# Three moved steps in an mLSTM and feed-forward kernel: chunk 3's mask, the copies of b, and the last piece of w_out

## The chip, the cores and the metric

The kernel runs on one core of a Trainium2 chip. The metric is the device time of one launch in microseconds (us). PE is TensorE, DVE is VectorE, ACT is ScalarE, POOL is GpSimd and SP is the engine that only issues transfers.

## The reference, cut to what matters

Two blocks follow each other. The first is a recurrent cell over 4 batches of 8 heads, 768 steps, head width 40. The second is a feed-forward block on its 3072 rows of 320 numbers:

```python
for t in range(S):
    m_new = np.maximum(f_gate[:, :, t] + m, i_gate[:, :, t])
    f_stab = np.exp(f_gate[:, :, t] + m - m_new)
    i_stab = np.exp(i_gate[:, :, t] - m_new)
    m = m_new
    C = f_stab[:, :, None, None] * C + i_stab[:, :, None, None] * np.einsum('bhd,bhe->bhde', vt, kt)
    n = f_stab[:, :, None] * n + i_stab[:, :, None] * kt
    h_tilde = np.einsum('bhde,bhe->bhd', C, qt)
    nq = np.einsum('bhd,bhd->bh', n, qt)[:, :, None]
    denom = np.maximum(np.abs(nq), 1.0)
    o = 1.0 / (1.0 + np.exp(-o_gate[:, :, t]))
    y[:, :, t] = o * h_tilde / denom
...
h = np.maximum(x @ w_in, 0.0)
return (h * h @ w_out).astype(np.float32)
```

Here `x` is `y` with the heads laid side by side (320 columns), `w_in` is 320 x 2048 and `w_out` is 2048 x 320. Both weights arrive as 64-bit numbers.

## The kernel before, in words

**Chunks.** The 3072 rows are cut into 24 chunks of 128 steps (6 chunks in each batch). A chunk is computed in a parallel form. Its scores k·q (`scores`) are multiplied by a matrix of weights `W` = exp(A + b), where A is the running sum of the log decays and b a number for each key; the product is `P` (`weighted`, line 552). `P` times the values, plus the state C of the chunks before, gives the numerators (`attend`, later `attend_begin` and `attend_end`), which are divided by the denominators (`normalise`, later `normalise_turned`).

**How W is made.** `load_A` brings A, spread over all partitions, into the tile `A_bc`. `mask` (line 425) lets GpSimd fill the places where the key is later than the query with -1e30. `weigh` then runs eight exponentials on ScalarE (line 467) and at last `values` multiplies the values by a column of W on GpSimd (`vw`, line 487). From chunk 8 on another layout is used, where the exponentials (line 461) take b from `b_R`. That is `b_T` with its halves of partitions exchanged, made by four ScalarE copies (line 1200).

**Weights.** `w_in` and `w_out` arrive in 18 pieces: pieces 0 to 9 are of `w_in`, 10 to 17 of `w_out`. A piece goes through the class `Rounding`. `fetch` loads it, `words` runs two ScalarE activations on it (`mag`, line 211, and `low`, line 213), and `join` runs three VectorE instructions (lines 222, 226, 227) and one GpSimd addition (line 231), then fetches another piece if one is left. `step` is `words` for the next piece and `join` for the oldest one.

**Two phases, one order written out by hand.** Every engine carries out its instructions in the order in which the program names them; no scheduler moves them.

- The first phase is the loop over `u`, from 0 to 7 (line 1137). Two values of `u` belong to one chunk s = 2 + u // 2: the even one does `scores`, `weighted` and `weigh(s + 1)`; the odd one does `attend`, `normalise` and the transposes of chunk s + 1. In each `u` a part of the first feed-forward product runs (`ffn1`, lines 799 and 810) into PSUM banks named `h_ps`, three of which exist. The next `u` begins with `relu_half` (line 823), which empties two of them. Joins of weight pieces fill in between: piece 4 in `u` = 0, pieces 5, 6 and 7 in `u` = 1.
- The second phase is the loop over the list `parts`, counted by `n` (line 1217); chunk s = 6 + n // 4 is spread over four values of `n`. It forms both feed-forward products with seven products of blocks instead of eight (`ffn1_begin`, `ffn1_open`, `ffn1_rows`, `ffn1_close`, `ffn2_fast`), except for the first two chunks of rows, which take the plain `ffn2` (line 836). `ffn1_begin` in `n` = 0 multiplies one block into each of two banks (line 966), lets ScalarE copy them (`r_sb`, line 979) and multiplies a second block on top. In `n` = 4 come the scores and `P` of chunk 7, and half of `ffn2` on the first rows. In `n` = 5 come `attend_begin(7)` and `attend_end(7)`, and between the two a one-element VectorE instruction (line 628) that TensorE waits for; then the other half of that product. At the start of `n` = 5 the buffers of `Rounding` are given back and `T` and `S` take their place; `T` holds differences of blocks of `w_out` (lines 864 to 871).

`LAST` tells for `n` = 0 to 4 how many pieces must have been joined by the end of that part.

Of the kernel before, what the change touches and what calls it, by code (L numbers as in the profile page):

```python
# [29 lines left out]
def kernel(  # L30
# [27 lines left out]
    nc = tc.nc  # L58
# [4 lines left out]
    PR = H // 2  # L63
# [190 lines left out]
    b_T = consts.tile([P, B, NB, H], F32)  # L254
    eA_T = consts.tile([P, B, NB, H], F32)
    b_R = consts.tile([P, B, NB, 2, PR], F32)
# [44 lines left out]
    HALVES = slice(0, DP), slice(DP, 2 * DP)  # L301
# [148 lines left out]
    def weigh(s, masked=False):  # L450
        b, c = divmod(s, NB)
        d = st[s]
        A, n = d["A"], H // len(d["A"])
        d["W"] = flat_c[:, H * P * (s % 2) : H * P * (s % 2 + 1)].rearrange("p (h t) -> p h t", t=P) if s < W_IN else A[0]
        if s < X_SQ:
            d["dec"] = prep.tile([P, H], F32, name="dec")
        if len(A) == 1 and not masked:
            mask(s)
        for x in range(PR if s >= ROT else 0):
            for own, to in enumerate((slice(DP, P), slice(P, 2 * P))):  # L460
                nc.scalar.activation(  # L461
                    A[0][:, x, to], A[0][:, x, to], AF.Exp, bias=b_R[:, b, c, own, x : x + 1],
                )
        for i in range(len(A) if s < ROT else 0):
            hh = slice(i * n, (i + 1) * n)
            for h in range(n):
                nc.scalar.activation(
                    d["W"][:, i * n + h, :], A[i][:, h, :], AF.Exp, bias=b_T[:, b, c, i * n + h : i * n + h + 1],
                )
            if s < X_SQ:  # L470
                nc.scalar.activation(d["dec"][:, hh], A[i][:, :, P - 1], AF.Exp)
        values(s)
# [346 lines left out]
    def relu_half():  # L819
        if "half" in st:  # L820
            hs, g4 = st.pop("half")
            for i, h in enumerate(hs):
                nc.scalar.activation(g4[:, :, i, :], h[:], AF.Relu)
            st.setdefault("relu", []).append(g4)
# [214 lines left out]
    def ffn1_square():  # L1039
        if "open" in st:  # L1040
# [4 lines left out]
            nc.scalar.activation(g4[:, :, :, P0], g4[:, :, :, P0], AF.Square)  # L1045
            nc.scalar.activation(g4[:, :, :, P1], g4[:, :, :, P1], AF.Square)

    def do(f, s):
        if 0 <= s < NT:
            f(s)  # L1050
# [86 lines left out]
    for u in range(8):  # L1137
        s = 2 + u // 2
        relu_half()
        if u % 2 == 0:  # L1140
            if u == 0:
                ffn1(0, 0)
            else:
                turn_rows(s - 1)
                scores(s)
                ffn1(u // 4, u % 4)
            if u == 2:
                rounding.words()
            weighted(s)
            if u == 0:  # L1150
                rounding.step()
            if u == 2:
                mask(s + 1)
                rounding.join()
                rounding.join()
                weigh(s + 1, masked=True)
                rounding.words()
            else:
                weigh(s + 1)
                square_half()  # L1160
        else:
            load_A(s + 2)
            for r in {1: (4,), 3: (5, 6), 5: (7,), 7: ()}[u]:
                load(r)
            if u == 5:
                for r in range(4, 8):
                    half_tanh(r)
            attend(s)
            if u == 3:
                square_half()  # L1170
            rounding.join()
            normalise(s)
            for r in {5: (8,), 7: (9,)}.get(u, ()):
                load(r)
            for r in {5: (7,), 7: (8,)}.get(u, ()):
                pair_up(r)
            if u > 4:
                load_o(2 * s)
                load_o(2 * s + 1)
            transposes(s + 1)  # L1180
            rounding.words()
            ffn1(u // 4, u % 4)
            square_half()
        if u < 4:
            load_o(4 + u)
        while rounding.done < NEXT[u]:
            rounding.step()
        if u in WIN_SUMS:
            sums_of_win(WIN_SUMS[u])
# [4 lines left out]

    for m in range(2):
        for own in range(2):
            x = PR * (m ^ own ^ 1)
            nc.scalar.copy(b_R[HALVES[m], :, :, own], b_T[HALVES[1 - own], :, :, x : x + PR])  # L1200
    spread_slots(1)
    banks.close()
    ps_h = ctx.enter_context(tc.tile_pool(name="ps_h", bufs=5, space=PSUM))
# [6 lines left out]
    for g in range(1, NG):  # L1210
        parts += [(2, g, i) for i in range(4)]
        if g + 2 < NG:
            parts += [(1, g + 2, i) for i in range(4)]
    LAST = (17, 17, 18, 18, 18)
    assert LAST[-1] == len(pieces)

    for n, (which, g, i) in enumerate(parts):
        s, at = 6 + n // 4, n % 4
        if n == 5:
            brought.close()  # L1220
            late = ctx.enter_context(tc.tile_pool(name="late", bufs=1, side="right"))
        even = s >= 8 and s % 2 == 0
        fast = which == 1
        if at == 0:
            if s < 8 or even:
                do(scores, s)
            if even:
                do(turn_kq, s + 1)
            if s < 8 or even:
                do(weighted, s)  # L1230
        if at == 1:
            do(attend_begin, s)
            if even:
                do(lambda s: scores(s, ("h", "h")), s + 1)
            if fast:
                ffn1_rows(g, 0, True)
            do(attend_end, s)
            do(decays, s + 1)
            do(mask, s + 1)
            if n > 4 and not even and not fast:  # L1240
                do(turn_kq, s + 1)
            do(decay_C, s + 1)
            if s > X_SQ and not fast and not even:
                do(turn_squares, s - 1)
            do(store_num, s)
            do(load_num, s)
            do(load_squares, s + 2)
            if even:
                do(load_A, s + 2)
        if 5 <= n < 8:  # L1250
            sums_of_weights(n - 5)
        if n == 6:
            sums(1, slice(0, NPAIR), (1, 2))
        if n == 8:
            sums_of_weights(3)
            sums(1, slice(0, NPAIR), (3,))
        if n == 9:
            sums(1, slice(0, NPAIR), (4,))
        if which == 2 and i == 3 and g == NG - 2:
            sums(g + 1, slice(0, NPAIR), (2,))  # L1260
        if which == 2 and g > 1 and i < 2:
            sums(g, slice(0, NPAIR), (3 + i,))
        if n == 0:
            ffn1_begin(g)
            sums_of_x(g)
            sums_of_win(2)
        if at == 3 and s >= 8 and s % 2 == 0 and s // 2 - 1 < NG:
            sums_of_x(s // 2 - 1)
        if at == 2 and not fast:
            if even:  # L1270
                do(turn_squares, s - 1)
            if n > 4:
                do(scale_q, s + 1)
        if at == 3:
            if s % 4 == 3:
                for r in range(s + 1, min(s + 5, NT)):
                    half_tanh(r)
        if fast:
            if i % 2:
                ffn1_close(g, i // 2, i == 1)  # L1280
                if at == 1 and g > 2:
                    do(turn_kq, s + 1)
                    do(turn_squares, s - 1)
            else:
                ffn1_open(g, i // 2)
                if i == 0 and g > 2:
                    sums(g - 1, slice(0, NPAIR), (2,))
            if at == 2 and g > 2:
                do(scale_q, s + 1)
        elif g == 0:  # L1290
            ffn2(g, *divmod(i, 2))
        else:
            ffn2_fast(g, i)
        if at == 2:
            do(lambda s: weigh(s, masked=True), s + 1)
            ffn1_square()
            if n < 4:
                do(turn_kq, s + 1)
                do(scale_q, s + 1)
            if even:  # L1300
                do(weighted, s + 1)
            do(normalise_turned, s)
            do(store_rows, s)
            if not even:
                do(load_A, s + 2)
            if s > 6:
                do(load_o, s + 5)
            do(load_rows, s)
            if s == 6:
                do(pair_up, s + 3)  # L1310
        if s > 6 and at == (3 if even else 2):
            do(pair_up, s + 3)
        if s > 6 and at == 3:
            if s == 7:
                load(s + 3)
            do(load, s + 4)
        if n in (9, 25):
            spread_slots(2 + n // 25)
        if at == 0:
            ffn1_square()  # L1320
        if n < 5:
            while rounding.done < LAST[n]:
                rounding.step()
# [30 lines left out]
```

## Time and profile before

| what | value |
|---|---|
| median of 3 runs | 500.82 us (500.54 to 502.58) |
| the profiled execution | 498.15 us, of which 496.4 us is the span from its first to its last instruction |
| TensorE clock granted | 1.000 |
| PE busy | 487.0 us (98%) |
| DVE, ACT, POOL busy | 346.3, 241.3, 224.5 us |

The span is the time from the first to the last instruction of the profiled execution; 1.75 us lie outside it. The median of the timed runs is 2.67 us above the profiled execution, so differences are worked out inside the profile and then set against the median. A row of the timeline gives start, duration, engine, line, operation and operands; in square brackets stands how long the engine was idle before it, and what ended that wait. Rows of one engine can overlap by about 0.1 us, because an instruction starts while its predecessor finishes.

### The profile page before, as it was taken

The numbers are of one execution on the slowest core, as the hardware profiler recorded it, in microseconds if no ns is written. First come the engines' busy times: TensorE is split into PE (matmuls) and PEld (weight loads), VectorE is DVE, ScalarE is ACT, GpSimd is POOL, SyncE is SP. The second block draws the span as 40 slices with busy tenths as digits, with TensorE's granted clock in tenths as the row PEclk, the third lists the DMA queues.
The fourth block names the chain that finished last, engine by engine and source line by source line (L and its number), as shares of the span: only waits on it lengthen the run. The fifth ranks groups of instructions, "written<-read, shape, count | busy, mean of one in ns | idle before, by whom it ended". The sixth has DMA issues, their size and how long they took to land.

```text
span 496.4 us, 15227 instructions
## 1 busy us (share of the span) xinstructions
PE 487.0 (98%) x6169; PEld 452.5 (91%) x6169; DVE 346.3 (70%) x700; ACT 241.3 (49%) x530; POOL 224.5 (45%) x317
## 2 busy tenths in 40 slices
PE   9999999999999999999999999999999999999997
PEld 4877878897799999999999999999999999999997
DVE  8598969868977677767866866866866956735441
ACT  3657888754612551581561670561861560423300
POOL 3265744531489458458549438448544030020000
PEclk9999999999999999999999999999999999999999
DMA  9999797756597597688678578677766532200000
GB/s 188 207 229 219 238 217 159 208 90 129 117 188 156 128 174 181 124 152 176 138 144 180 130 145 176 153 138 161 155 125 142 116 74 80 55 15 15 3 26 28
DMA packets 196167, 68.02 MB, mean 137 GB/s; under 512 B 158704, under 2 KB 186064, under 8 KB 196096
## 3 DMA queue, kind: packets, MB, share of 16 engines
q1 hardware_dynamic: 190560, 57.50, 55.9%
q0 software_dynamic: 5440, 9.34, 8.0%
q8 instruction: 49, 0.80, 0.7%
q10 hardware_dynamic: 96, 0.20, 0.2%
q14 instruction: 22, 0.18, 0.1%
HBM read 54.71 MB, written 18.01 MB: 146 GB/s over the span
## 4 chain that ended last, share of the span: by engine, by line
PE 90%; DVE 4%; ACT 2%; issue 1%; DMA 1%; POOL 1%; SPq 0%; DVEq 0%; POOLq 0%; ACTq 0%
PE h_ps L890 35%; PE h_ps L966 24%; PE h_ps L1015 7%; PE h_ps L799 4%; PE h_ps L836 3%; PE numT L655 2%; PE numT L636 2%; PE hp L575 2%; PE idle L1059 1%; PE h_ps L810 1%; PE numT L666 1%; PE tp L530 1%; PE h_ps L530 1%; PE tp L504 1%; PE tp L538 1%
## 5 line engine op out<-in xcount | busy, mean ns | idle before, releaser
L890 PE MATMUL h_ps<-T,S 128*128 128x160 f32 x352 | 51.7, 300 | 0.0
L996 ACT COPY r_sb<-h_ps 128x512 f32<-128x512 f32 x18 | 10.5, 585 | 83.7 <-PE h_ps L966 83.7
L890 PEld LDWEIGHTS h_ps<-T,S 128*128 128x128 f32 x352 | 48.9, 190 | 0.4 <-ACT g_c L1032 0.2
L890 PE MATMUL h_ps<-w_out,g 128*128 128x160 f32 x336 | 49.2, 303 | 0.0
L890 PEld LDWEIGHTS h_ps<-w_out,g 128*128 128x128 f32 x336 | 46.1, 190 | 1.3 <-issue 0.7
L906 DVE TENSOR_TENSOR y_sb<-y_sb,h_ps 128x160 f32<-128x160 f32 x44 | 14.1, 320 | 47.5 <-PE h_ps L890 47.5
L431 POOL TENSOR_SCALAR_AFFINE_SELECT A_bc<-A_bc 64x512 f32<-64x512 f32 x32 | 25.2, 788 | 47.0 <-ACT kq L448 40.7
L966 PE MATMUL h_ps<-xT,w_in 128*128 128x128 f32 x320 | 43.0, 278 | 0.8 <-ACT r_sb L979 0.8
L966 PE MATMUL h_ps<-lent_t,w_in 128*128 128x128 f32 x320 | 42.2, 275 | 0.0
L966 PEld LDWEIGHTS h_ps<-xT,w_in 128*128 128x128 f32 x320 | 38.9, 192 | 2.4 <-issue 1.0
L1015 PE MATMUL h_ps<-xT,w_in 64*64 64x128 f32 x960 | 39.1, 272 | 0.0
L966 PEld LDWEIGHTS h_ps<-lent_t,w_in 128*128 128x128 f32 x320 | 38.9, 192 | 0.2 <-issue 0.2
L966 PE MATMUL h_ps<-lent_t 128*128 128x128 f32 x320 | 39.0, 275 | 0.0
L966 PEld LDWEIGHTS h_ps<-lent_t 128*128 128x128 f32 x320 | 37.3, 192 | 0.0
L461 ACT ACTIVATE A_bc<-A_bc,b_R 128x64 f32<-128x64 f32 (+1 forms) x128 | 35.7, 361 | 1.0 <-POOL A_bc L431 0.5
L1015 PEld LDWEIGHTS h_ps<-xT,w_in 64*64 64x64 f32 x960 | 34.8, 133 | 1.3
L340 POOL DMA_DIRECT2D va<-in_v_dram x56 | 34.3, 619 | 2.5 <-DMA va<-in_v_dram 1.4
L686 DVE STREAM_TRANSPOSE tn<-numT 128x256 f32<-128x256 f32 x36 | 14.0, 428 | 28.6 <-PE numT L636 19.8
L481 POOL TENSOR_TENSOR vw<-va,A_bc 128x328 f32<-128x328 f32 x13 | 10.7, 822 | 50.6 <-ACT A_bc L461 50.5
L799 PE MATMUL h_ps<-xT,w_in 128*128 128x256 f32 x128 | 29.9, 384 | 1.7 <-POOL w_in L231 1.1
L958 POOL TENSOR_TENSOR lent_t<-xT 128x128 f32<-128x128 f32 (+1 forms) x18 | 13.0, 738 | 38.5 <-DVE xT L769 38.5
L799 PEld LDWEIGHTS h_ps<-xT,w_in 128*128 128x128 f32 x128 | 23.5, 190 | 5.8 <-POOL w_in L231 1.5
(200 smaller groups left out, 1191.0 us busy)
## 6 DMA issues: line engine op xcount, KB each, us to landing
A_bc<-a_slots SPq DMA_DIRECT2D x32, 256.0 KB, 4.7
num_rows<-tn SPq DMA_DIRECT2D x18, 256.0 KB, 2.2
kq<-num_rows SPq DMA_DIRECT2D x72, 64.0 KB, 2.0
raw<-in_moe_w_out_dram SPq DMA_DIRECT2D x7, 640.0 KB, 4.2
kqT<-kq_rows SPq DMA_DIRECT2D x34, 128.0 KB, 3.0
og<-in_o_gate_dram SPq DMA_DIRECT2D x24, 160.0 KB, 5.3
out_dram<-y_sb SPq DMA_DIRECT2D x24, 160.0 KB, 3.1
raw<-in_moe_w_in_dram SPq DMA_DIRECT2D x7, 512.0 KB, 5.6
```

Source lines behind the costliest of these rows:

```text
L340: eng.dma_start(dst[HALVES[n], PR * (1 - late_keys) : PR * (2 - late_keys)], src[HALVES[late_keys], PR * m : PR * (m + 1)],)
L431: nc.gpsimd.affine_select(part, part, compare_op=ALU.is_ge, fill=-1e30, base=0, pattern=[[0, PR], [0, 2], [1, DP]], channel_multiplier=-1,)
L461: nc.scalar.activation(A[0][:, x, to], A[0][:, x, to], AF.Exp, bias=b_R[:, b, c, own, x : x + 1],)
L481: nc.gpsimd.tensor_tensor(d["vw"][:].rearrange("p (own x) d -> p own x d", own=2), d["va"][:].rearrange("p (own x) d -> p own x d", own=2) ...
L686: nc.vector.transpose(to[:, 2 * m : 2 * m + 2], d["numT"][m].rearrange("p c t -> p (c t)"))
L799: nc.tensor.matmul(hs[i][:, n, :], lhsT=w_in[:, a, fb * P : (fb + 1) * P], rhs=xT[:, :, a, :], start=(n == 0 and a == 0), stop=False,)
L836: nc.tensor.matmul(o_ps, lhsT=st["g2", g][:, fb, j * P : (j + 1) * P], rhs=w_out[:, fb, :], start=(fb == 0), stop=(fb == NF - 1),)
L890: nc.tensor.matmul(to, lhsT=lhsT[:, p], rhs=rhs[:, p, :], start=(start and p == 0), stop=(p == NPAIR - 1), skip_group_check=True,)
L906: add = lambda to, a, b: nc.vector.tensor_tensor(to, a, b, op=ALU.add)
L958: sub = lambda to, a, b: eng.tensor_tensor(to, a, b, op=ALU.subtract)
L966: nc.tensor.matmul(to[:, n, :], lhsT=lhsT[:, 4 * q + n, :], rhs=rhs, start=(start and n == 0), stop=True, skip_group_check=True,)
L1015: nc.tensor.matmul(to[cols, n, :], lhsT=w_in2[rows, 4 * q + n, cols], rhs=rhs, start=(start and n == 0), stop=True, skip_group_check=True,)
```

## The change

There are three edits. (1) In `u` = 0 the mask of chunk 3 is issued ahead of `rounding.step()`, so on GpSimd it stands ahead of the addition of piece 4; `weigh(3)` is then called with `masked=True`. (2) The four copies to `b_R` leave the place between the two phases and become the function `turn_halves`, called in `n` = 3 after that part's products. (3) `LAST` changes in `n` = 2 and `n` = 3, so that the last piece of `w_out` (17) is joined at the end of `n` = 4 instead of the end of `n` = 2.

In the built program the engines' orders differ in just these places. On POOL the mask stands before one addition (`w_in`, 128x512) instead of after it. On ACT the four copies stand after the activation of line 1032 in `n` = 3 instead of ahead of the two copies `r_sb`. On DVE the three instructions of piece 17 stand after the two multiplications of `P` of chunk 7 (line 552) instead of ahead of the four additions of `ffn1_close` (lines 1033 to 1036). The orders on PE and SP are the same as before; no instruction is added or removed.

```diff
+    def turn_halves():
+        for m in range(2):
+            for own in range(2):
+                x = PR * (m ^ own ^ 1)
+                nc.scalar.copy(b_R[HALVES[m], :, :, own], b_T[HALVES[1 - own], :, :, x : x + PR])
...
             weighted(s)
             if u == 0:
+                mask(s + 1)
                 rounding.step()
...
             else:
-                weigh(s + 1)
+                weigh(s + 1, masked=(u == 0))
                 square_half()
...
-    for m in range(2):
-        for own in range(2):
-            x = PR * (m ^ own ^ 1)
-            nc.scalar.copy(b_R[HALVES[m], :, :, own], b_T[HALVES[1 - own], :, :, x : x + PR])
     spread_slots(1)
...
-    LAST = (17, 17, 18, 18, 18)
+    LAST = (17, 17, 17, 17, 18)
...
+        if n == 3:
+            turn_halves()
         if n in (9, 25):
```

## Prediction

> **What bounds the kernel now.** The first page lines to read are the span and the busy times.
>
> ```profile
> span 496.4 us, 15227 instructions
> ...
> PE 487.0 (98%) x6169; PEld 452.5 (91%) x6169; DVE 346.3 (70%) x700; ACT 241.3 (49%) x530; POOL 224.5 (45%) x317
> ```
>
> TensorE is busy for all but 9.4 us. A gain without fewer matmuls must come out of those, so the second question is where they lie. The table of stretches (length, then busy us and count for PE, PEld, DVE, ACT, POOL, clock, DMA share, GB/s) answers:
>
> ```profile
> 54.00:97.00 43.00, 41.83 (x299) 35.20 (x299) 35.45 (x57) 36.11 (x73) 21.33 (x17) 1.00 0.94 208
> 97.00:125.00 28.00, 26.38 (x433) 23.35 (x434) 20.59 (x44) 16.01 (x30) 8.79 (x11) 1.00 0.58 109
> 125.00:220.00 95.00, 95.00 (x1339) 89.04 (x1340) 71.39 (x148) 45.10 (x108) 60.58 (x93) 1.00 0.77 154
> ```
>
> From 125 us to the products' end PE never stops. What is won or lost before 125 therefore moves the end one for one. Third, the waits of PE:
>
> ```profile
> PE tp L777 <- ACT g L823: 1.2, 1, 1.2
> PE h_ps L799 <- POOL w_in L231: 1.1, 1, 1.1
> ...
> PE h_ps L966 <- ACT r_sb L979: 0.8, 1, 0.8
> PE h_ps L799 <- ACT g L823: 0.6, 1, 0.6
> PE numT L636 <- DVE A_bc L552: 0.5, 1, 0.5
> ...
> PE numT L666 <- DVE kq L628: 0.3, 1, 0.3
> ```
>
> Five of these six lie behind work that the change moves; the 1.2 (at 65.39 us) does not. The chain of waits shows what stands ahead of them (start, us, what):
>
> ```profile
> 38.88 1.09 issue
> 39.97 1.36 POOL A_bc L425
> ...
> 45.81 0.58 ACT mag L211
> ...
> 49.37 1.33 POOL w_in L231
> ...
> 98.77 0.17 ACT b_R L1200
> ...
> 99.71 3.85 PE h_ps L966 x32
> ...
> 118.43 0.83 DVE mag L227
> ...
> 121.64 0.61 DVE A_bc L552
> ```
>
> All three moved things (the mask, the copies to b_R, the last join) are on it.
>
> **What the Trainium skill says.** "SBUF — State Buffer", section "SBUF: two separate sides": VectorE and GpSimd share a pair of ports under an exclusive lock held for a whole instruction; a VectorE instruction in a two-port mode or with two SBUF inputs takes it. The trace agrees: the shift of line 226 takes 0.43 us alone and 1.38 beside an addition (49.60). "Perfetto Trace Analysis", section "Sequencer Loop": an engine's instruction waits for its semaphores in the engine's own queue, so what stands behind it waits too. The trace agrees: ACT was idle 3.69 us before 41.35, with the exponentials and all behind them waiting for the mask.
>
> **Part 1, the mask.** It is one GpSimd instruction: 1.09 us at 28.13, 1.35 at 39.97. It waits for A of chunk 3, issued by SP at 31.17 and landing 6.5 us later (its DMA row), at 37.7. GpSimd is free from 37.13 and idle until 38.75 (1.62, waiting for line 227 of piece 4). So the mask runs from 37.8 to 39.0 instead of 39.97 to 41.32, and the exponentials start at 39.1 instead of 41.35: ScalarE gains 2.3 us. Behind the new wait stands the addition of piece 4. VectorE's line 227 of that piece (37.91, 0.69) will probably be held by the mask until 39.0, ending at 39.6, and the addition then ends at 40.9 instead of 40.02. PE reads piece 4 at 41.91: no loss. SP's fetch of piece 8 (38.67), released by the same line 227, slips by 1 us with the loads of chunk 4 behind it: piece 8 lands by about 46 and ScalarE wants it at 48.91; A of chunk 4 lands by about 47 and its mask stands at 53.08.
>
> What it frees: (a) the wait at 44.43 for line 823. The 16 matmuls from 41.91 took 4.51 us; the same group at 59.53 took 3.62. The relu now ends by 42.2 and PE wants the bank at about 43.7: 0.85 us. (b) the wait at 50.75 for the addition of piece 6, ready at 50.69, which followed from ScalarE's `mag` at 45.71, itself behind the exponentials. PE's two matmuls at 48.99 would be followed at about 49.45 without it: 1.3 us with the start-up. Freed of everything this is 2.1 us, of which PE's own waits name 1.7; I take 1.9 as the ceiling. But ScalarE is not the only limit. GpSimd's vw, Cd, C_sb and the addition of piece 5 (0.74 + 0.73 + 0.88 + 1.27 = 3.6 us alone) stood at 43.88 to 47.75, mostly beside an idle VectorE; now they fall at 41.7, on top of VectorE's normalise of chunk 2 and piece 6 (0.17 + 0.17 + 0.44 + 0.49 + 0.20 + 0.42 + 0.43 + 0.69 = 3.0). By turns from the end of piece 5's line 227 at 42.3 that is 6.6 us, less the overlap of starts. From 28.13 to 31.30 six such instructions with 3.83 us alone took 3.17: 0.11 less each. Twelve: 6.6 - 1.3 = 5.3, line 227 of piece 6 ends at 47.6 to 48.2 (the later when vw is ahead of piece 5's end), the addition 1.4 later at 49.0 to 49.6, against 50.7. So **1.5 us of the 1.9** is taken; bounds 0.3 (no overlap of starts) and 1.9. PE wants normalise's output at 46.6 and has it at about then. The wait at 65.39 stays: it is VectorE's `x_sb` (line 746, to 65.24), whose chain back to 49 has no idle time, so it comes earlier by the same 1.5.
>
> **Part 2, the copies.** Four ScalarE copies, 1.11 us from 97.93, stand ahead of the two r_sb copies (99.07, 0.59 for the first). PE's first block matmuls end by about 97.8 and 98.75. Without the copies the first r_sb copy runs 97.93 to 98.5, the second from 98.85 to 99.45, and PE goes on at 98.75 and 99.65 with both at hand. PE resumes at 98.75 to 98.9 instead of 99.71: **0.9 us** (0.8 to 1.0). At their new place ScalarE sits idle 5.86 us (115.82 to 121.68, waiting for line 1036), and the first reader of b_R is the exponential at 129.95: nothing there. Without that cover they would delay squares that PE reads only after 138.
>
> **Part 3, the last join.** Three VectorE instructions, 117.38 to 119.17 (1.79 us), leave the path to line 552; piece 17 has no piece after it to fetch, so no transfer moves. P of chunk 7 is then ready at 121.05 instead of 122.84, before PE asks (121.35): the 0.5 and what follows it go, about 0.85 us. What is late next: VectorE then runs the join until 122.85, and line 628, which PE waits for, stands behind it; PE alone would have it at 122.5. So line 628 goes from 123.63 to 122.87: **0.75 us** (0.3 to 1.3; the low end if the addition takes the lock first. At 106.09 line 628 followed a join just so and took 0.16). The addition runs to about 124.45 on an idle GpSimd; PE wants its rows of w_out twelve matmuls of 0.27 into the stretch at 124.1, at 127.4, and T wants them at 126.8.
>
> Sum: 1.5 + 0.9 + 0.75 = 3.15. The profiled execution is 498.15 us and would become 495.0; the median of the runs stands 2.67 above it, so 500.82 - 3.15 = **497.7 us**.
>
> **Rivals.** (A) All named stalls go, without a loss at the port: 1.9 + 0.9 + 0.75 = 3.55, 497.3. For it: ScalarE gains 2.3. Against it: 49.60 and 62.66 (0.17 became 1.46) show the lock at work in this stage. (B) The mask's gain turns into a wait at the port: GpSimd's early products stretch normalise of chunk 2 and piece 6 so far that the addition of piece 6 comes as late as before. Left are 0.3 + 0.9 + 0.75 = 1.95, or 1.65 with none: 498.9 to 499.2. For it: 28.32, where line 745 took 1.24 instead of 0.44 beside a mask. (C) Slower: GpSimd stands at the mask until A of chunk 3 lands, with piece 4's addition queued behind. Addition and mask need 2.6 us before PE's 41.9, so landing after 39.2 stalls PE one for one; with the other parts' 1.65 to make up and 2.5 more, it takes a landing after 43.4, 12 us after issue: 503.4. Against it: loads of A land after 5.5 to 6.6 us. That the change does not do what it says is excluded by the built order; that the b copies cost nothing before is what the 0.8 in the list of waits speaks against.
>
> **Numbers.** 0.5% (2.5 us) is about what a measurement of this kernel can tell from no change. The forecast has 0.50 (of it 0.46 below 498.3), A 0.17, B 0.25, C 0.08. Faster: 0.46 + 0.17 = 0.63; same: 0.04 + 0.25 = 0.29; slower: 0.08. The range runs from 496.2 (A with part 3's upper bound of 1.3, and 0.5 for the spread of the median) to 499.8 (B with part 3's low end 0.3 and 0.2 of that spread); it leaves out C and little else. The forecast's own range is 497.0 to 498.5.
>
> **What would show it.** Right: the mask starts at 37.8, line 823's wait at 44.4 is gone, the 14 matmuls of line 799 start near 49.2; PE's wait for r_sb is gone; line 628 stands right after line 227 of piece 17. Wrong: x_sb of chunk 2 later than 47 us, new PE waits at line 777, any wait of PE after 122, or a line 628 of over a microsecond.

## The result and the profile after

| | before | after |
|---|---|---|
| median of 22 runs each, on one chip | 499.75 us (497.25 to 504.0) | 497.32 us (494.8 to 502.25) |
| ratio, 95% interval | | 0.9938 (0.9916 to 0.9960) |
| profiled execution (span) | 498.15 (496.4) us | 497.72 (496.0) us |

The kernel is faster by 0.6%; of 500 us the ratio makes 3.1 us (2.0 to 4.2). The ratio leaves out executions in a slower state, which last some per cent longer, and so isn't the quotient of the two medians (0.9951). A second comparison gave 0.9939. The forecast, 497.7 against 500.82, was a ratio of 0.9938. Such an agreement of a sum says little before its parts are seen.

The page of the changed kernel, span and busy times:

```profile
span 496.0 us, 15226 instructions
...
PE 486.8 (98%) x6169; PEld 452.8 (91%) x6169; DVE 346.6 (70%) x700; ACT 241.6 (49%) x530; POOL 224.6 (45%) x317
```

The work is the same. The profiled execution gained only 0.4 us, far less than the runs; the one before lies below its kernel's median of 499.75, the one after above its own of 497.32. The table of stretches of the changed kernel (length, then busy us and count for PE, PEld, DVE, ACT, POOL, clock, DMA share, GB/s) tells where PE's idle time now lies:

```profile
54.00:97.00 43.00, 41.35 (x296) 34.90 (x295) 35.51 (x56) 35.56 (x71) 21.89 (x16) 1.00 0.96 201
97.00:125.00 28.00, 27.39 (x436) 24.22 (x435) 22.38 (x50) 16.79 (x33) 9.73 (x14) 1.00 0.60 121
...
220.00:300.00 80.00, 79.16 (x1189) 76.94 (x1188) 55.86 (x123) 38.02 (x88) 48.83 (x75) 1.00 0.74 148
```

From 97 to 125 PE lost 1.62 us before and loses 0.61 now. From 220 to 300, where PE was busy all 80 us before, it now loses 0.84. And from 54 to 97 it loses 1.65 instead of 1.17. The list of PE's waits names what is behind this:

```profile
PE numT L666 <- DVE kq L628: 0.8, 2, 0.6
PE numT L636 <- DVE A_bc L552: 0.7, 1, 0.7
PE h_ps L799 <- POOL w_in L231: 0.7, 1, 0.7
PE tp L777 <- DVE x_sb L747: 0.5, 1, 0.5
```

The waits for r_sb and for line 823 ahead of line 799 are gone, and the one for piece 6 fell from 1.1 to 0.7. The wait for line 552 has the same name as before, but the row lies at 288.3, not in chunk 7. The wait for line 747 is in a new place, 64.75.

The three parts in the timeline of the changed kernel. First the mask:

```profile
36.80 1.28 POOL L425 TENSOR_SCALAR_AFFINE_SELECT A_bc<-A_bc 128x1024 f32<-128x1024 f32 x1
38.12 2.45 ACT L467 ACTIVATE g_c<-A_bc,b_T 128x128 f32<-128x128 f32 x8 [0.76 <-POOL A_bc L425]
39.24 1.27 POOL L231 TENSOR_TENSOR w_in<-mag,low 128x512 int32<-128x512 int32 x1 [1.16 <-PE dC L568]
...
47.01 0.69 DVE L227 SCALAR_TENSOR_TENSOR mag<-raw,mag 128x512 int32<-128x512 int32 x1
47.85 1.31 POOL L231 TENSOR_TENSOR w_in<-mag,low 128x512 int32<-128x512 int32 x1 [3.04 <-DVE mag L227]
...
49.22 3.29 PE L799 MATMUL h_ps<-xT,w_in 128*128 128x256 f32 x14 [0.71 <-POOL w_in L231]
```

The mask runs 3.2 us earlier than before, and so do the exponentials (0.28 of it is this profile's earlier start, seen below); the addition of piece 4 behind it is done at 40.51, ahead of the matmuls at 41.63. Then the copies and the last join:

```profile
96.00 3.88 PE L966 MATMUL h_ps<-xT,w_in 128*128 128x128 f32 x32
...
120.13 0.82 DVE L227 SCALAR_TENSOR_TENSOR mag<-raw,mag 128x640 int32<-128x640 int32 x1
...
120.98 0.16 DVE L628 TENSOR_SCALAR kq<-numT 1x1 f32<-1x1 f32 x1
```

The first 32 matmuls of line 966 now run in one row, without the 0.8 between the blocks. Line 628 stands directly behind the join of piece 17.

### The profile page after: what moved, and what is told of

It reads as the page before. It is cut to its first block, busy times and chain, and to the rows that moved or that the text cites. A ratio compares the mean times of both kernels' runs of the same rounds, so it can differ in the third digit from the quotient of the medians.

```text
span 496.0 us, 15226 instructions
## 1 busy us (share of the span) xinstructions
PE 486.8 (98%) x6169; PEld 452.8 (91%) x6169; DVE 346.6 (70%) x700; ACT 241.6 (49%) x530; POOL 224.6 (45%) x317
## 4 chain that ended last, share of the span: by engine, by line
PE 84%; DVE 10%; DMA 2%; issue 1%; SPq 1%; POOL 0%; DVEq 0%; POOLq 0%
PE h_ps L890 34%; PE h_ps L966 23%; PE h_ps L1015 6%; PE h_ps L799 3%; PE h_ps L836 3%; PE numT L655 2%; PE numT L636 2%; DVE mag L226 2%; PE hp L575 1%; PE idle L1065 1%; PE numT L666 1%; PE tp L538 1%; DMA kqT<-kq_rows 1%; DVE mag L227 1%; PE tp L530 1%
## 5 line engine op out<-in xcount | busy, mean ns | idle before, releaser
L890 PE MATMUL h_ps<-w_out,g 128*128 128x160 f32 x336 | 49.2, 303 | 0.0
L906 DVE TENSOR_TENSOR y_sb<-y_sb,h_ps 128x160 f32<-128x160 f32 x44 | 14.1, 320 | 47.6 <-PE h_ps L890 47.6
L431 POOL TENSOR_SCALAR_AFFINE_SELECT A_bc<-A_bc 64x512 f32<-64x512 f32 x32 | 23.2, 726 | 43.5 <-ACT kq L448 42.2
L966 PEld LDWEIGHTS h_ps<-xT,w_in 128*128 128x128 f32 x320 | 38.9, 192 | 1.4 <-issue 1.0
L890 PE MATMUL h_ps<-w_out,g_c 128*128 128x160 f32 x192 | 28.0, 302 | 0.0
```

The costliest lines, as they stand in the source:

```text
L431: nc.gpsimd.affine_select(part, part, compare_op=ALU.is_ge, fill=-1e30, base=0, pattern=[[0, PR], [0, 2], [1, DP]], channel_multiplier=-1,)
L890: nc.tensor.matmul(to, lhsT=lhsT[:, p], rhs=rhs[:, p, :], start=(start and p == 0), stop=(p == NPAIR - 1), skip_group_check=True,)
L906: add = lambda to, a, b: nc.vector.tensor_tensor(to, a, b, op=ALU.add)
L966: nc.tensor.matmul(to[:, n, :], lhsT=lhsT[:, 4 * q + n, :], rhs=rhs, start=(start and n == 0), stop=True, skip_group_check=True,)
```

## The experiments

Chip times of one kernel scatter by some us, so a part worth 1 us is hard to see in them. Each experiment was therefore read in two ways: by the ratio of the timed runs, and by intervals in its profile between groups of matmuls that every kernel has. Interval I runs from the start of the 16 matmuls of line 799 at 41.9 to the 14 behind piece 6 (part 1). Interval II runs from those 14 to the scores of chunk 4 at 65, and III from there to the first matmul of line 966. IV ends at the first 16 matmuls of line 836 and holds the r_sb copies (part 2). V goes from those to the 48 matmuls of line 836 (part 3). In us:

| kernel | I | II | III | IV | V |
|---|---|---|---|---|---|
| before | 8.84 | 15.08 | 31.00 | 20.02 | 8.04 |
| after | 7.59 | 15.79 | 30.99 | 18.98 | 7.26 |
| part 1 alone | 8.21 | 15.85 | 32.69 | 20.01 | 8.21 |
| part 2 alone | 8.82 | 15.88 | 32.63 | 18.97 | 8.40 |
| part 3 alone | 8.83 | 15.94 | 32.64 | 20.01 | 7.25 |
| parts 1 and 2 | 7.58 | 15.08 | 31.00 | 18.98 | 8.00 |
| parts 1 and 3 | 7.59 | 15.09 | 30.99 | 20.02 | 6.94 |
| parts 2 and 3 | 8.82 | 15.08 | 31.00 | 18.98 | 7.26 |

### Each part alone, and the whole again

Part 1 alone keeps the two lines of `mask(s + 1)` and `masked=(u == 0)`; part 2 alone keeps `turn_halves` and its call; part 3 alone keeps `LAST`.

> The kernel before with part 1 alone (chunk 3's mask ahead of piece 4's addition). Landmarks of PE in the kernel before: the 14 matmuls of line 799 at 50.75 us, the scores of chunk 4 (line 538) at 65.83, the 48 matmuls of line 836 at 124.96. Theory (the mask pays, and its gain is cut twice by the port that VectorE and GpSimd share): the first landmark comes 1.2 to 1.5 us earlier; where the mask of chunk 5 then meets the copy of line 747, PE waits about 0.5 longer at line 777 and only 0.6 to 0.9 is left from the second landmark on; the time falls by 0.6 to 1.3. Rival (nothing is lost later, the small rest of the forecast is scatter): 1.5 at all three landmarks, time lower by 1.5. Rival (the mask's gain does not last): below 0.3 at 124.96.

> The kernel before with part 2 alone (the four copies to b_R in n = 3). Theory: PE's wait for r_sb (0.8) is gone, nothing takes its place, the first landmarks stay and the 48 matmuls of line 836 come 0.9 to 1.0 us earlier than 124.96; time lower by 0.9. Rival (VectorE or the loads of the second phase fill the gap): the wait for r_sb goes, but less than 0.5 is left at 124.96.

> The kernel before with part 3 alone (piece 17 joined at the end of n = 4). Theory: PE's wait for line 552 (0.5) goes, its wait for line 628 grows from 0.3 to about 0.6 because the join's three instructions stand ahead of it, and the 48 matmuls of line 836 come 0.75 us earlier. Rival (line 628 takes the place of the whole wait): under 0.3 earlier. Time lower by 0.75 or by under 0.3.

> The changed kernel once more. Its first profile shows PE waiting after 125 us, 0.7 at 287 us and 0.2 at 324, behind kqT<-kq_rows loads that landed late (VectorE idle 2.0 us at 286.6 where before it was 0.4), so that the 2.65 us won at 125 had shrunk to 0.4 at the end of that execution. Theory (those late loads are an execution's chance, found in any of these kernels): this profile has other such waits, or none, and the timed runs are about 2.5 us below before. Rival (the earlier start brings the loads too late, so the changed kernel always waits there): again waits at about 287 and 324 us, of 1 us or more together, which the kernel before and the single parts do not show.

Measured ratios: part 1 0.9975 (0.9938 to 1.0013), part 2 0.9983 (0.9961 to 1.0005), part 3 1.0003 (0.9970 to 1.0035), the whole 0.9939 (0.9916 to 0.9963). Only the whole is told apart from no change. The parts' intervals hold the forecast shares (0.9970, 0.9982, 0.9985) and nothing as well; the times alone thus decide nothing on the parts.

The profiles do. Interval IV is 1.04 shorter in every kernel with part 2 and in no other: that is part 2. Interval V is 0.8 shorter with part 3 alone, 0.8 with parts 2 and 3, 0.8 and 1.0 with the whole, 1.1 with parts 1 and 3. It scatters more than the others: over all fourteen profiles of this study it is 6.9 to 7.3 with part 3 and 7.6 to 8.4 without, two ranges that don't meet. With part 2 alone it is 0.36 longer, because there PE waits for line 552 0.9 instead of 0.5; part 2 had been expected to bring no new wait. With parts 1 and 2, where part 3 is missing as well, that wait is 0.5 and V is 8.00, so the loss isn't shown to be part 2's.

Part 1 alone showed 8.21 in interval I, a gain of 0.63, half of what it has in company and of the 1.2 to 1.5 expected. In that profile the front ran 0.9 earlier, A of chunk 3 landed only at 37.67, and the mask waited 0.92 for it; the GpSimd instructions behind it then fell beside VectorE's lines 745 and 746, which took 1.13 and 1.45 instead of 0.44 and 0.49. In the seven other profiles with part 1 and all else in place, it has its 1.25.

The repeat of the whole decided its question for neither side. PE waited 0.44 at 288 and not at 324, less than the rival's 1 us; but VectorE again waited 1.68 for the load at 286.71, and of a lead of 2.73 at the 48 matmuls 0.28 was left at the last product.

### The parts in pairs

> Parts 1 and 2 together, without part 3. So far each part alone moved the median of the executions with a full clock (0.999 or more) by only 0.2 to 0.6 us (before 499.0, part 1 498.5, part 2 498.8, part 3 498.9 in four executions), the whole change by 3.4 (495.6). Theory (the parts add up as PE's landmarks say, and the sum of the single times, 1.1, is low by scatter): 1.2 from part 1 and 0.7 from part 2, which alone loses 0.3 to the wait for line 552: 1.9, so 497.1. Rival (the parts need each other: what one wins is waited for again unless all three are there): at most 1.1 below before, so 497.9 or more.

> Parts 2 and 3 together, without part 1. Theory (parts add up; with part 3 the wait for line 552 is gone, so part 2 keeps its whole 1.05): from the first matmuls of line 966 to the 48 of line 836 it is 26.2 us instead of 28.06, the time 1.8 below before, 497.2 at the full clock. Rival (the parts need each other): the same interval, but at most 0.6 below before in time, 498.4 or more.

> Parts 1 and 3 together, without part 2. Theory (parts add up): 1.2 + 0.8 = 2.0 below before, 497.0 at the full clock; PE's wait for r_sb stays at 0.8. Rival (the parts need each other): at most 0.8 below before, 498.2 or more.

Measured: 0.9958 (0.9931 to 0.9985), 0.9964 (0.9934 to 0.9995) and 0.9962 (0.9933 to 0.9992). Each pair is faster by about 1.9 us, and parts 2 and 3 without the mask as well. (The single gains quoted above add up to 0.8, not 1.1.) The times that were forecast at the full clock, about 497.1, were missed: the medians were 498.71, 498.46 and 498.73. But these runs were made on another chip than those of the single parts, and there the kernel before had 500.37 and not 499.0. The pairs lie 1.6 to 1.9 below it; the rivals allowed at most 1.1, 0.6 and 0.8. For parts 1 and 3 the medians of all executions lie only 0.2 apart (501.25 and 501.42), so this pair rests on its ratio and its profile. That the parts bring something only all together is refuted; they add up, as far as 0.3% of resolution tells.

### What sets interval I: the port or ScalarE

On the changed kernel, with the old state left out of chunk 2: two of the four GpSimd instructions between the additions of pieces 4 and 6 disappear (1.6 us alone), and nothing on ScalarE's way changes.

```diff
-            if c > 0:
+            if c > 0 and s != 2:
```

> The changed kernel without GpSimd's two state instructions of chunk 2 (lines 589 and 594; the old state is left out of the new one there), 1.6 us of GpSimd work that falls beside VectorE's normalise. It tests what limits part 1. From the matmuls of line 799 of u = 1 to the 14 matmuls that wait for piece 6 it is 8.84 us in the kernel before and 7.59 and 7.58 in two executions of the changed one; without any wait it would be 6.65. Theory (the shared port): VectorE reaches line 227 of piece 6 about 1 us earlier and the interval falls to 6.7 to 6.9. Rival (ScalarE's activations of piece 6, or its arrival, limit it): 7.6 as before.

Interval I fell from 7.59 to 6.77, within what the port would give. The row of its PE's timeline behind the scores of chunk 3, and the third matmul in it by itself:

```profile
47.29 3.88 PE L799 MATMUL h_ps<-xT,w_in 128*128 128x256 f32 x16
...
47.88 0.48 PE L799 MATMUL h_ps<-xT,w_in 128*128 128x256 f32 x1
```

The 16 matmuls are one row of 3.88, no longer 2 and 14 with a wait of 0.71 between them (the 14 begin at 47.88). In both kernels VectorE runs the same instructions without idle time from line 227 of piece 5 to line 227 of piece 6; they take 5.99 us in the changed kernel and 5.16 here. The 0.7 that part 1 leaves thus comes from GpSimd's instructions taking turns with VectorE. ScalarE, which this kernel leaves as it was, is not the limit, and neither is GpSimd's own queue: in the changed kernel it stood idle for 3.04 us ahead of the addition of piece 6. The time of this kernel (one run, 499.46) says nothing of that, since its clock dropped later on (last section).

### The copies twice

On the kernel before, the four copies to b_R are made twice (`for twice in range(2):` around the loop).

> The kernel before with the four copies to b_R made twice at their old place: 1.11 us more of ScalarE work. From the first matmuls of line 966 to the 16 matmuls of line 836 it is 20.02 us in the kernel before and 18.98 in the changed one. Theory (ScalarE's copies stand on PE's path one for one): 21.1 us, and PE's wait for r_sb 1.9 instead of 0.8. Rival (the wait has another cause, the drain of the first phase's banks, or part of the copies is hidden): 20.0 to 20.5.

The list of waits of this kernel's PE begins with

```profile
PE h_ps L966 <- ACT r_sb L979: 2.0, 1, 2.0
```

against 0.8 before. The copies are eight in 2.33 us instead of four in 1.11. The wait grew by 1.2, as much as the copies: what stands ahead of the r_sb copies costs PE one for one, and part 2 saved the 0.8 and what hung on it (1.04). Interval IV is 22.85, of which 1.7 is a drop of the clock (last section); the rest, 21.1, is 1.1 above the kernel before. PE then reaches line 552 so late that it doesn't wait for it, and interval V is 7.63. One run took 501.75.

### The mask of chunk 5 behind an addition

The wait for line 747 that the profile after shows at 64.75 was new. Its two neighbours in the timeline of the changed kernel:

```profile
63.41 1.24 POOL L425 TENSOR_SCALAR_AFFINE_SELECT A_bc<-A_bc 128x1024 f32<-128x1024 f32 x1 [0.85 <-DMA A_bc<-a_rows]
...
63.73 0.97 DVE L747 COPY x_sb<-x_sb 128x64 f32<-128x64 f32 x1
...
64.75 0.33 PE L777 MATMUL tp<-ident,x_sb 128*128 128x128 f32 x1 [0.50 <-DVE x_sb L747]
```

and in the second profile of the same kernel:

```profile
64.56 0.20 DVE L747 COPY x_sb<-x_sb 128x64 f32<-128x64 f32 x1
...
64.76 1.09 POOL L425 TENSOR_SCALAR_AFFINE_SELECT A_bc<-A_bc 128x1024 f32<-128x1024 f32 x1 [1.38 <-DMA A_bc<-a_rows]
```

The mask of chunk 5 starts when A lands. If that is just ahead of the copy, the copy takes 0.97 instead of 0.20 and PE waits. Interval II shows the two outcomes, 15.1 or 15.8 to 15.9 (and 16.0 with the old state left out); the three single parts hit the late one, the kernel before and all the pairs missed it, and the changed kernel hit it once and missed it once. So it is not the change that makes it, but the instant at which a load lands. The next kernel is the changed one with that mask behind the addition of piece 11, in the even branch for u = 4:

```diff
             else:
+                if u == 4:
+                    rounding.step()
                 weigh(s + 1, masked=(u == 0))
```

> The changed kernel with the mask of chunk 5 issued behind the addition of piece 11 (rounding.step() ahead of weigh in u = 4). In the executions so far that mask, waiting for its load, started between 0.4 us ahead of and 0.2 us behind VectorE's copy of line 747; ahead of it, the copy took 1.0 us instead of 0.2 and PE waited 0.5 to 0.65 for it (changed kernel once, the three single parts each once), behind it not (kernel before once, changed kernel once). Theory (a toss-up at the port in every kernel of this study): line 747 takes 0.2, the interval from the 14 matmuls of line 799 to the scores of chunk 4 is 15.1 us instead of 15.8, and the time is 0.3 to 0.5 us below the changed kernel's. Rival (the later mask pushes ScalarE's exponentials into PE's way): a new wait of PE for line 823 or 507 between 74 and 82 us, and no gain.

> The changed kernel with the mask of chunk 5 behind the addition of piece 11, once more, because its first six executions (median 494.81) are few. Theory (the copy of line 747 is always free of the mask): line 747 takes 0.2 again, PE waits at line 777 of chunk 3 only for line 746, and the median at the full clock is 494.7 to 495.3, 0.3 to 0.9 below the changed kernel's 495.6. Rival (six lucky executions): 495.6 or more.

The mask stood at 70.26 instead of 63.41, line 747 took 0.20 and 0.19, and interval II was 15.09 and 15.08, with no new wait behind it. The ratios were 0.9903 (0.9872 to 0.9934; 6 runs) and 0.9936 (0.9909 to 0.9964; 22 runs). The second forecast of the time failed: the median at the full clock was 497.75, on the chip of the pairs, 2.6 below the kernel before there. The collision is gone, but the gain in time over the changed kernel isn't shown: the second ratio is the same as its own.

### The join behind line 628

On the changed kernel, the join of piece 17 moved behind line 628: `LAST = (17,) * 5`, and in n = 5 `rounding.step()` after `attend_begin`, with the buffers' return behind it.

> The changed kernel with the join of piece 17 moved once more, between attend_begin(7) and attend_end(7) in n = 5, so behind line 628. Theory (in the changed kernel line 628 stands behind the join, which sets PE's wait of 0.6): that wait falls to about 0.3, the interval from the 16 to the 48 matmuls of line 836 falls from 7.26 to about 6.9, the time by 0.3. Rival (the addition of piece 17 now comes too late for the last rows of w_out in n = 5): a wait of PE for line 231 inside the 48 matmuls, and no gain.

Interval V fell to 6.93 and the wait for line 628 to 0.3, as expected, and nobody waited for the later addition. That the moved join did this isn't shown: parts 1 and 3, and the mask of chunk 5 later in its second profile, have the same 6.94 and 6.93 and the same 0.3 with the join ahead of line 628. And the ratio was 0.9990 (0.9960 to 1.0020): the 0.3 of gain did not arrive, and against the ratio of the changed kernel, which was not run on this chip, some 2.6 us are missing. Of its 14 timed executions 13 had a mean clock below 0.999, and in its profile PE waits 1.4 us at 177 for line 552, behind a load `kqT<-kq_rows` that took 5.52 to land. Whether the moved join brings this about stays open.

## Why the prediction was right

**The path.** Right in kind: what was won was won as waits of PE ahead of 125, at the three steps named. In the profile after, the 48 matmuls of line 836 start at 122.24 against 124.89 before: 2.65 us. Of that, 0.28 was there before 32 us, 1.25, 1.04 and 0.78 are the three parts, and 0.71 was lost in interval II.

**Part 1.** Forecast 1.5, measured 1.25, and 0.63 where the mask had to wait for A. The mechanism was right: what is left of PE's wait is the port. The mask stood at 36.80, not 37.8, because A was issued at 30.25 instead of 31.17 and landed within 5.9 us instead of 6.5; so ScalarE gained 3.2 instead of 2.3. That line 227 of piece 6 nevertheless ended at 47.70, as forecast (47.6 to 48.2), and the 14 matmuls stood at 49.22 ("near 49.2"), is in part luck. The twelve instructions did not all follow 42.3: `vw` and `Cd` ran from 40.64 on, beside the join of piece 5, whose line 227 ended at 42.82. Two instructions of normalise (lines 737 and 741, 0.69 together in the profile before) were not in the count. And 0.28 is the front. The forecast's own case, a mask 4.1 us ahead of the 16 matmuls of line 799 (37.8 and 41.91), occurs in no profile: seven have it 4.6 to 4.8 ahead and gain 1.25 to 1.3, one has it 3.4 ahead and gains 0.6.

**Part 2.** Forecast 0.9, measured 1.04. **Part 3.** Forecast 0.75, measured 0.8 to 1.1; line 628 followed the join in 0.16 us, and PE waits 0.61 for it. The sum is 3.1 to 3.4 against 3.15, with part 1 a little under and part 2 a little over the forecast.

**The rivals.** A (3.55, no loss at the port) has the same time within the interval of the ratio, so the time doesn't decide against it; the wait of 0.7 that is left, and its end when GpSimd has less to do, exclude it. B left part 1 with 0.3 at most; 1.25 was measured, and 0.63 at worst. C wanted a landing of A after 43.4; it landed by 36.8.

**What failed.** Two steps, and what came of both stood in the forecast's own list of signs of being wrong (new waits at line 777, waits of PE after 122). "It comes earlier by the same 1.5", of the wait at 65.39, held only where the mask of chunk 5 didn't come first: in the profile after, 0.7 of the gain was lost there. The forecast had looked back from the wait and found a chain without idle time; it hadn't asked which other engine would start an instruction at that moment.

And "from 125 us to the products' end PE never stops … one for one". In the profiles it did stop. The chain that ended last in the changed kernel (start, us, what):

```profile
279.93 1.91 PE h_ps L1015 x64
...
317.85 5.31 DMA kqT<-kq_rows
...
327.73 11.06 PE h_ps L890 x80
```

and the same groups of matmuls in the chain of the kernel before:

```profile
282.57 1.91 PE h_ps L1015 x64
...
328.15 11.06 PE h_ps L890 x80
```

The lead is 2.64 at 280 and 0.42 at 328, and stays so to the end. Of the loss, 1.6 falls between 283 and 307 and 0.6 behind the slow load of 5.31 at 318. At the first place VectorE waits for such a load, too:

```profile
286.58 1.25 DVE L370 STREAM_TRANSPOSE kqT<-kqT 128x1024 f32<-128x1024 f32 x1 [2.00 <-DMA kqT<-kq_rows]
```

Before, this row stood at 286.71 with 0.39 of waiting: the load came in at nearly the same instant, although all around it was 2.6 earlier. It was issued earlier, too (line 363 began at 278.29 instead of 280.44), but the slowest of the four transfers took 6.6 us to land instead of 4.5. Of the seven profiles that reach the 48 matmuls by 122.4 us, six take 2.2 us or more longer from there to the last product than the kernel before (drops of the clock apart), the seventh (the mask of chunk 5 later) 0.3. The six others that come later take 0.0 to 2.1 longer. That seventh shows that the lead can last: it is 3.40 at the 48 matmuls and 3.10 at the last product, with the load issued at 277.14 and landed in 4.1 us. Neither profile of the changed kernel itself carries its lead to the end. Yet the timed runs of the change show 3.1 and those of the pairs 1.9, so these losses cannot be the rule in them; the step from the won waits to the time is thus inferred, not seen. Whether an early arrival makes late loads likelier stays open; no kernel here took these loads away.

## What to carry to other kernels

The gain of work moved up on one engine ended here at the next shared resource, the port of VectorE and GpSimd. A count of the instructions that fall side by side there told the size to within 0.3 us where the mask's load was early, and not where it was late. A step that is "not touched by the change" still needs the question what starts on another engine at that moment. And where parts are each worth less than a run's scatter, intervals between the same groups of matmuls in several profiles tell them apart, while their times don't.

## What was not expected of the hardware

In a stretch of some profiles the TensorE clock falls to half for a few us. The table of stretches of part 1 alone, microsecond by microsecond:

```profile
64.00:65.00 1.00, 0.44 (x3) 0.17 (x2) 0.77 (x1) 0.00 (x0) 0.72 (x1) 1.00 1.56 129
...
66.00:67.00 1.00, 1.00 (x9) 0.83 (x6) 0.72 (x2) 1.00 (x4) 0.00 (x0) 0.88 1.52 149
67.00:68.00 1.00, 1.00 (x4) 0.74 (x4) 0.97 (x3) 1.00 (x5) 0.00 (x0) 0.50 1.54 135
...
70.00:71.00 1.00, 1.00 (x6) 0.82 (x5) 0.00 (x0) 0.42 (x1) 1.00 (x2) 0.92 1.00 361
```

Between 62.7 and 64.8 PE stood still for 1.16 and 0.56, with 0.4 of work between. From about 66.8 on the clock is at half for 3.4 us, and the 16 matmuls of line 799 at 66.17 take 5.41 instead of 3.62. Added up, the clock lost 1.70 us, and interval III is longer by just that (32.69). Nine of the fourteen profiles have such a drop between 60 and 490 us. It costs 1.70 or 1.71, or 3.41 where it lasts twice as long (the old state left out; the join behind line 628), and each time it follows within some 2 us on gaps of PE that come to between 1.4 and 2.0. The profiles without one have gaps up to 1.2, but for the changed kernel's 1.15 and 0.50. So the gap alone doesn't decide. Nor does it otherwise: with the copies twice a gap of 1.47 at 42.5 had no drop behind it, and two profiles (the changed kernel's second, and the second with the mask of chunk 5 later) have one at 14 us, in the front, behind gaps of no more than 0.44.

The Trainium skill, page "TensorE: Matmul & The Clock Gate", section "What's actually happening", states half the clock after at least one idle window of about 3.4 us, and that the window runs freely. The half and the length agree (3.4 us at half are 1.7 lost), and a free window would explain why 1.65 passed in one profile and 1.44 didn't in another. The condition doesn't agree: no profile has PE idle for 3.4 us at a stretch in this span, and gaps of about half a window came before these drops. The end of the program speaks for the shorter time as well: behind the last matmul the clock falls to half after 2.1 to 5.2 us in the fourteen profiles, in seven of them after less than 3. That the gaps cause them is an association and wasn't tested by itself. If they do, a wait of 1.7 us costs another 1.7. It would also give the mask of chunk 5 a weight beyond its 0.7: where that mask is kept behind the addition, 24 of 28 executions kept a mean clock of 0.999 or more; in the changed kernel 24 of 44. The two were not run on the same chips, but on the chips of the former the kernel before kept it in 48 of 94.
